# Pooled attention and a token/channel mixer on one core: the head and all step plans in a new order

## The chip, the cores and the metric

The kernel runs on one core of one Trainium2 chip. A core has five engines that run side by side, each working through its own instructions in program order: TensorE (PE, matmuls), VectorE (DVE), ScalarE (ACT), GpSimd (POOL) and SyncE (SP, which here only issues DMAs). They wait for each other through semaphores. Matmul results go to PSUM (eight banks), everything else lies in SBUF. The metric is the device time of one execution in microseconds (us); the median of three runs stands for a kernel.

## The reference

Attention over keys and values that are averaged over 8 neighbours, then a mixer over the sequence and one over the channels:

```python
# q, k, v: (8, 8, 576, 64) = batch, heads, sequence, head size
k_p = k.reshape(B, H, S // 8, 8, D).mean(axis=3)          # 72 pooled keys
v_p = v.reshape(B, H, S // 8, 8, D).mean(axis=3)
attn = softmax(q @ k_p.T / sqrt(D))                       # 576 x 72 for each head
x = (attn @ v_p)                                          # to (8, 576, 512): batch, sequence, channels
h = relu(x.T @ w_tok1) @ w_tok2                           # over the sequence: 576 -> 256 -> 576
u = x + h.T
out = u + relu(u @ w_ch1) @ w_ch2                         # over the channels: 512 -> 1536 -> 512
```

## The kernel before

**What is computed where.** A batch is 576 rows of 512 channels: four chunks of 128 rows, and a tail of 64 that two batches share. The last stage, over the channels, is cut into nine *units*: unit n takes the four full chunks of batch n (n = 0 to 7), unit 8 all the tails. A unit (`unit_fast`) is first 12 tiles of u @ w_ch1 (`l1_tile`, 4 matmuls of 128x512 each, then a ReLU on ACT into `GT`), then seven products with w_ch2, 12 matmuls of 128x256 each, in which the 2x2 blocks of the matrix product are combined from fewer products with the help of sums: `=1` to `=4` (`g_sums`, sums of halves of `GT`) and `w0` to `w3` (`weight_sum`, sums of halves of w_ch2, once, in unit 0). The sums are single DVE instructions of 128x1536. Each product is read out of PSUM by DVE (`plus`); an output is stored by SP.

**The steps of a batch.** While unit n runs, the attention and the token mixer of the batches after it are worked in, as small steps (`batch_steps`):

- `lk`, `lv`, `lq`: the loads of K, V and Q, DMAs that POOL issues (two, two and one).
- `K0`, `K1`, `V0`, `V1`: pooling of four heads on POOL, three instructions each; `v1` is the same on DVE; `kpool`, `vpool0`, `vpool1` are the same by matmuls with an identity, read out by DVE.
- `Q0`, `Q1`: transposes of Q on DVE. `kpT`: transposes of the pooled keys on PE, read out by ACT.
- `s0`, `s1`, `s2`: scores (16 matmuls, in two PSUM buffers of the pool `ps_two`), then two exponentials on ACT.
- `av0` to `av4`: weighted values (8 matmuls in one buffer of `ps_two`), then a reciprocal and a product on DVE; `av4` is the tail.
- `at0`, `at1`: first half of the token mixer, 5 matmuls, ReLU on ACT. `u0` to `u4`: second half, 2 matmuls (4 in `u4`), plus x on DVE.
- For batches 0 to 2 `t0` to `t3` turn u over on PE, and ACT reads it out. For batches 3 to 7 this goes through memory instead: `M0`, `M2`, `M4` write pairs of chunks to memory, `M` (four DMAs) and `MT` (two) read them back in another layout, all issued by SP, and `T0` to `T5` finish with a transpose on DVE.

`l1_tile`, `at`, `u`, `kpT`, `t`, the pooling by matmul and the products take their PSUM bank from one list of four (`take`, `give`): a bank goes to whoever is next in program order, and that one waits until the former reader is done.

**What sets the order.** The order of all instructions is written out by hand in two tables. `HEAD` is the list of steps before unit 0: the first loads (`LkA` to `Lc2c`: parts A, B and T of K and V of batch 0, Q, the weights t1, t2, c1 and c2, and batch 1), batch 0's attention by finer steps (`kp`, `kt`, `q`, `o`, `e`, `a`, `m`: pooled keys, their transposes, queries, odd and even scores, weighted values, token mixer), `p0` and `p1` (a permutation of w_tok2 on ACT and on POOL), and `d1` to `d4`, which are one to four spare matmuls of 128x512 whose result nobody reads. `PLAN` has one dictionary for each unit: a unit has 45 slots (24 half tiles of `l1_tile`, 21 thirds of a product), and after slot i the steps listed under i are issued. Position in the table sets the place in the queue of every engine that the step uses; engines don't wait for each other because of it, only for data.

**Gates.** `g` in a plan is a one-element memset on DVE and a one-element copy of it on POOL. So POOL goes no further until DVE has come there; and since the next memset overwrites what the copy reads, DVE at the next gate waits until POOL has done the copy of the gate before.

```python
def gate():
    nc.vector.memset(flag[:, 0:1], 0.0)
    nc.gpsimd.tensor_copy(out=flag[:, 1:2], in_=flag[:, 0:1])

def unit(n, at):
    ...
    for i, _ in enumerate(unit_fast(n, st)):
        for s in at.get(i, "").split():
            ...
```

In the lists after the heading of the change, `2.K1` under 27 in the first dictionary means: step K1 of batch 2, after slot 27 of unit 0.

Of the kernel before, what the change touches and what calls it, by code (L numbers as in the profile page):

```python
# [32 lines left out]


# [745 lines left out]
```

## Time and profile before

| | |
|---|---|
| median of three runs | 271.05 us (268.42 to 271.4) |
| the profiled execution, its own time | 269.83 us |
| its span, first to last instruction | 268.0 us |
| mean granted TensorE clock | 0.998 |
| first matmul, last product's start | 1.19 us, 263.06 us |
| unit 0's first l1 matmul | 27.18 us |
| DMA traffic of the core | 34.29 MB, 128 GB/s on average, some 200 GB/s until 59 us |

The profile is of one execution. A row of the timeline has the start, the length, the engine, the line of the kernel, the operation, what is written from what, the shape and the count; in brackets stand the idle time of the engine just before and what ended it. Names of tiles leave out buffer numbers: `p1a` to `p1d` are the four banks of the list, `p` a buffer of `ps_two`, `area` the `GT` sums, `flag` the gate, `mem` the memory that batches 3 to 7 go through and `v` what is read back from it. The lines: L514 is an l1 matmul and L518 its ReLU, L580 a product and L623 its readout, L542 and L554 the sums, L297 scores and L306 their exponentials, L376 an `av` with L380 and L381 on DVE, L390 an `at`, L407 and L412 `u` with L413 on DVE, L421 a `t`, L222 `kpT`, L174 to L180 pooling, L118 and L128 loads, L431 spills, L443 the reads back and L455 the DVE transposes, L676 a spare matmul, L709 and L710 the gate.

### The profile page before, as it was taken

What the parts mean: (1) busy time and instruction counts of PE and PEld (TensorE: products, weight loads), DVE (VectorE), ACT (ScalarE), POOL (GpSimd) and SP (SyncE); (2) the same over time, 40 slices, a digit from 0 to 9 for tenths busy, and PEclk for the clock granted to TensorE, in tenths of its full rate; (3) what the DMA queues carried; (4) which work ended last, traced back from release to release, by engine and by line L of the source; (5) the groups of instructions that cost most, each with busy time, mean ns of one, the idle gap of its engine ahead of it and who ended that gap; (6) DMA issues with size and microseconds to landing.
All of it is one profiled execution on the core that took longest, in us unless ns stands there. A gap on an engine that the chain in (4) does not pass through costs nothing. (4 is left out here: it accounts for less than half of the span.)

```text
span 268.0 us, 5292 instructions
## 1 busy us (share of the span) xinstructions
PE 254.6 (95%) x2091; PEld 159.1 (59%) x2113; DVE 177.7 (66%) x368; ACT 119.4 (45%) x196; POOL 148.3 (55%) x175
## 2 busy tenths in 40 slices
PE   7788999989989999999998999999999999999994
PEld 3674366754647645674486347754774486486483
DVE  5476359986699654994879836952796577175183
ACT  2454674039545556415740474265525412612700
POOL 8585324899997999899935892598400001000000
PEclk9999999999999999999999999999999999999999
DMA  7999999992099817699539721370326052603204
GB/s 153 189 206 201 206 206 208 207 201 57 2 150 155 170 36 148 142 217 235 175 85 167 203 81 39 43 205 0 116 45 158 30 163 48 156 0 88 71 0 157
DMA packets 31704, 34.29 MB, mean 128 GB/s; under 512 B 3136, under 2 KB 23744, under 8 KB 31680
## 3 DMA queue, kind: packets, MB, share of 16 engines
q0 software_dynamic: 17632, 17.64, 41.3%
q1 hardware_dynamic: 13632, 15.93, 20.7%
q10 hardware_dynamic: 416, 0.39, 0.4%
q8 instruction: 16, 0.26, 0.4%
q14 instruction: 8, 0.07, 0.1%
HBM read 38.99 MB, written 12.58 MB: 192 GB/s over the span
## 5 line engine op out<-in xcount | busy, mean ns | idle before, releaser
L514 PEld LDWEIGHTS <-w_ch 128*128 128x128 bf16 x432 | 39.3, 98 | 43.9 <-issue 3.2
L710 POOL COPY flag<-flag 1x1 f32<-1x1 f32 x45 | 10.8, 240 | 88.7 <-DVE flag L709 88.5
L580 PEld LDWEIGHTS <-area 128*128 128x128 bf16 x432 | 40.9, 98 | 9.4 <-issue 2.7
L306 ACT ACTIVATE ex<-p 72x768 bf16<-72x768 f32 x42 | 31.6, 806 | 22.5 <-PE p L297 22.5
L580 PEld LDWEIGHTS <-GT 128*128 128x128 bf16 x324 | 30.9, 98 | 7.8 <-issue 1.3
L175 POOL TENSOR_TENSOR t<-t 72x512 f32<-72x512 f32 x23 | 31.3, 1359 | 1.8
L514 PE MATMUL p1a<-uT,w_ch 128*128 128x512 bf16 x104 | 28.5, 379 | 0.3 <-issue 0.2
L518 ACT ACTIVATE GT<-p1a 128x512 bf16<-128x512 f32 x30 | 18.0, 599 | 19.4 <-PE p1a L514 19.3
L514 PE MATMUL p1d<-uT,w_ch 128*128 128x512 bf16 x95 | 25.8, 379 | 0.3
L174 POOL TENSOR_TENSOR t<-kr 72x1024 f32<-72x1024 bf16 x12 | 25.5, 2123 | 0.4
L518 ACT ACTIVATE GT<-p1d 128x512 bf16<-128x512 f32 x28 | 16.8, 599 | 17.7 <-PE p1d L514 11.7
L514 PE MATMUL p1c<-uT,w_ch 128*128 128x512 bf16 x87 | 24.2, 379 | 0.4 <-issue 0.2
L174 POOL TENSOR_TENSOR t<-vr 72x1024 f32<-72x1024 bf16 x11 | 23.3, 2118 | 0.5 <-DMA vr<-in_v_dram 0.3
L518 ACT ACTIVATE GT<-p1b 128x512 bf16<-128x512 f32 x24 | 14.4, 599 | 18.9 <-PE p1b L514 17.7
L514 PE MATMUL p1b<-uT,w_ch 128*128 128x512 bf16 x83 | 22.3, 379 | 0.1
L518 ACT ACTIVATE GT<-p1c 128x512 bf16<-128x512 f32 x26 | 15.6, 600 | 13.8 <-PE p1c L514 12.8
L381 DVE TENSOR_TENSOR x<-p,den 128x512 bf16<-128x512 f32 x28 | 19.4, 692 | 1.0
L376 PEld LDWEIGHTS <-ex 72*128 72x128 bf16 x280 | 13.3, 98 | 7.5 <-DVE x L381 2.1
L376 PE MATMUL p<-vp,ex 72*128 72x65 bf16 x280 | 14.9, 194 | 1.1 <-DVE x L381 0.8
L554 DVE TENSOR_TENSOR area<-GT 128x1536 bf16<-128x1536 bf16 x9 | 8.7, 963 | 9.4 <-ACT GT L518 9.3
L118 POOL DMA_DIRECT2D kr<-in_k_dram x17 | 11.0, 650 | 5.0 <-DMA w_ch<-in_moe_w_ch_dram 1.7
L455 DVE STREAM_TRANSPOSE uT<-v 128x256 uint32<-128x256 uint32 x20 | 8.2, 429 | 7.2 <-DMA v<-mem 7.2
(173 smaller groups left out, 464.2 us busy)
## 6 DMA issues: line engine op xcount, KB each, us to landing
out_dram<-o SPq DMA_DIRECT2D x32, 256.0 KB, 3.6
qb<-in_q_dram POOLq DMA_DIRECT2D x7, 576.0 KB, 8.9
kr<-in_k_dram POOLq DMA_DIRECT2D x7, 512.0 KB, 7.5
vr<-in_v_dram POOLq DMA_DIRECT2D x7, 512.0 KB, 12.3
w_ch<-in_moe_w_ch_dram POOLq DMA_DIRECT2D x5, 512.0 KB, 14.9
mem<-u SPq DMA_DIRECT2D x10, 256.0 KB, 2.2
v<-mem SPq DMA_DIRECT2D x20, 128.0 KB, 2.9
area<-in_q_dram SPq DMA_DIRECT2D x2, 288.0 KB, 3.1
```

Source lines behind the costliest of these rows:

```text
L118: nc.gpsimd.dma_start(out=t[j0:j1, h0:h1].rearrange("j h i d -> j h (i d)"), in_=src[b, h0:h1].rearrange("h (j i) d -> j h (i d)", i=POOL) ...
L174: eng.tensor_tensor(out=t4[:, 0:n], in0=t[:, hs, 0:4], in1=t[:, hs, 4:8], op=ALU.add)
L175: eng.tensor_tensor(out=t4[:, 0:n, 0:2], in0=t4[:, 0:n, 0:2], in1=t4[:, 0:n, 2:4], op=ALU.add)
L306: nc.scalar.activation(out=dst, in_=src, func=AF.Exp, scale=scale)
L376: nc.tensor.matmul(out=ps[:, h // 4, (h % 4) * (D + 1):(h % 4 + 1) * (D + 1)], lhsT=st["ex"][:, h * S + n0:h * S + n0 + P], rhs=st["vp"][: ...
L381: nc.vector.tensor_tensor(out=dst.rearrange("p (a h d) -> p a h d", a=2, d=D), in0=view[:, :, :, 0:D], in1=den[rows, :, :, None].broadcast ...
L455: nc.vector.transpose(out=dst.rearrange("f k n -> f (k n)").bitcast(U32).rearrange("f (k o a t) -> f o a k t", k=4, o=4, a=2)[:, o], in_=s ...
L514: nc.tensor.matmul(out=ps, lhsT=w_ch1[:, kk, m * P:(m + 1) * P], rhs=uT[kk], start=(kk == 0), stop=(kk == 3))
L518: nc.scalar.activation(out=GT[:, m, :], in_=ps, func=AF.Relu)
L554: nc.vector.tensor_tensor(out=S4[:, 0], in0=GT[:, f, hi], in1=GT[:, sec, hi], op=ALU.add)
L580: nc.tensor.matmul(out=ps[i] if split else ps[:, i], lhsT=chunk(u, i, a(m)), rhs=w(m), start=start and m == 0 and (i == 0 or split), stop= ...
L710: nc.gpsimd.tensor_copy(out=flag[:, 1:2], in_=flag[:, 0:1])
```

## The change

Both tables get new contents; no other line differs. `HEAD` has the same steps in another order, with 17 instead of 19 spare matmuls (12 instead of 14 of them ahead of the first step that needs K, `kp1`): LvT goes ahead of LkB, Lt2 ahead of LvB and Lt1, Lc1a and Lc1b ahead of Lk1 and Lq1, Lc2a ahead of Lc1d; kp0 and kp2 go ahead of their former neighbours kt1 and o1, o2 and p0 change places with others, and the `m`, `u` and `t` steps have a new order. `PLAN` has the same steps of each batch and the same sums in each unit, at other slots; 3.lk goes to the very start of unit 0, and the number of gates of units 1 to 8 goes from 4, 5, 6, 4, 5, 7, 6, 2 to 5, 6, 4, 4, 9, 11, 2, 1 (unit 0 has 6 in both).

```diff
--- before.py
+++ after.py
@@ -18,17 +18,17 @@
 SYNC = mybir.EngineType.SP
 
 
-HEAD = """LkA LkT LkB Lq LvA LvT LvB Lt1 Lt2 Lk1 Lq1 Lc1a Lc1b Lc1c p1 Lv1 Lc1d Lc2a Lc2b Lc2c d2 d3 c1 prep c0 d1 d2 d4 q1 d2 q0 kp1 kt1 kp0 o1 kp2 e1 kt0 kt2 o0 q3 e0 q2 d1 e3 o2 vpool0 e2 a02 a00 vpool1 o3 a04 a10 m03 m01 p0 m04 a12 m02 m10 m11 a14 m00 d1 m13 m12 m14 u1 u3 d2 u2 t1 u0 d1 t3 t2 t0 1.kpool"""
+HEAD = """LkA LkT LvT LkB Lq LvA Lt2 LvB Lt1 Lc1a Lc1b Lk1 Lq1 p1 Lc1c Lv1 Lc2a Lc1d Lc2b Lc2c c1 d3 d2 d2 prep d4 q1 c0 d1 q0 kp1 kp0 kt1 kp2 o1 kt0 e1 kt2 q3 o0 e0 q2 e3 vpool0 o3 e2 d2 a02 p0 a00 vpool1 o2 a04 d1 a10 m03 m04 a12 m01 d1 m02 m11 a14 m00 m10 m13 m12 m14 u3 u0 u1 d1 u2 t3 t0 t1 t2 1.kpool"""
 PLAN = [
-    {0: "2.lk 2.lv", 1: "1.kpT", 2: "1.Q1", 5: "1.Q0", 6: "1.s0", 10: "1.s1", 11: "g 1.vpool0", 12: "2.lq =3", 13: "3.lq 1.s2", 14: "1.vpool1", 15: "1.av1", 16: "1.av0 g", 17: "1.av2", 19: "1.av3", 20: "1.av4 w0", 22: "g", 23: "=1", 24: "1.at1 3.lk w1", 25: "=2", 26: "3.lv =4 1.at0 g w3", 27: "2.K1", 30: "2.K0", 31: "1.u0", 33: "g 1.u2", 34: "1.u1", 35: "w2", 37: "1.t0", 39: "1.u3", 41: "2.Q0", 42: "1.t3 2.V0", 43: "1.t1 1.t2", 44: "1.u4 g 2.kpT 2.Q1"},
-    {1: "3.Q0", 2: "2.s0", 3: "3.Q1", 6: "2.s2", 8: "3.K0", 11: "2.s1", 14: "3.K1", 15: "2.v1", 17: "2.av3", 18: "2.av0", 19: "2.av4", 21: "g 4.lq 2.av1", 22: "2.av2", 24: "5.lk g", 25: "3.V1 =1 =2 2.at0", 26: "3.kpT", 27: "2.at1", 29: "3.s0 2.u3 4.lk 2.u1", 30: "2.u2 4.Q0", 31: "3.s2", 32: "4.lv", 33: "2.t3", 34: "=4 g =3", 35: "2.u0", 36: "3.s1", 39: "2.t2", 40: "3.V0", 42: "2.t1 2.t0", 43: "g", 44: "3.av4"},
-    {1: "4.K0", 2: "g", 3: "3.av0 4.Q1 g", 4: "4.K1", 5: "3.av3", 9: "6.lk", 10: "3.av1", 11: "3.av2 g", 13: "4.V0 =3 3.at0", 14: "4.V1", 15: "3.at1", 16: "4.kpT 3.u0", 17: "3.u2 4.s2", 19: "3.u3", 21: "3.u1", 22: "3.M2", 23: "6.lq", 24: "3.M0 =1 5.lq", 25: "5.lv", 26: "3.M =2", 27: "g", 30: "4.s1", 31: "3.u4", 32: "4.s0 =4", 34: "3.T1", 35: "g", 36: "3.T0", 38: "6.lv", 39: "3.T3 4.av4 3.T2", 40: "4.av1", 41: "3.M4", 42: "4.av0", 44: "3.MT 5.Q0"},
-    {0: "4.av2", 4: "5.K1", 5: "5.K0", 6: "4.av3", 7: "g", 9: "5.Q1 4.at1", 10: "4.at0 5.kpT", 12: "4.u0 4.u2", 13: "6.Q0 5.s0", 14: "5.V0 4.u3", 16: "5.V1 4.M2", 17: "4.u1", 18: "=3", 19: "3.T5", 20: "3.T4", 21: "4.M0", 23: "=1 5.s1", 24: "g", 25: "=2 4.M", 27: "5.av1 g", 29: "7.lk", 30: "4.T1", 31: "4.T2 g", 32: "5.s2", 33: "=4", 34: "5.av0", 36: "7.lq", 37: "g 5.av3 g", 38: "5.av2", 40: "4.T3 5.av4", 43: "4.T0", 44: "5.at0 5.at1"},
-    {1: "6.Q1 5.u0 6.K0", 2: "6.K1", 3: "5.u1", 5: "5.u2 g 5.u4", 8: "g", 10: "5.u3", 13: "6.V1 5.M0", 14: "6.kpT 7.Q0", 15: "g", 17: "6.s0", 19: "5.M2 5.M", 20: "7.Q1", 23: "5.T3", 25: "=1 =2", 28: "6.s2", 29: "=4 5.T1 5.T2 6.V0", 32: "=3 5.T0", 33: "g", 36: "6.s1", 39: "7.lv", 43: "6.av4", 44: "6.av2"},
-    {2: "6.av0", 7: "7.K0", 11: "7.K1 g 6.av3", 13: "6.av1", 14: "g 7.V0", 15: "6.at1 6.at0", 18: "6.u0 6.u1", 19: "7.kpT", 20: "g", 22: "6.u3 7.V1 6.u2 7.s0", 25: "6.M2 6.M0", 26: "=1", 28: "=2 7.s1", 29: "=4", 30: "g", 32: "7.av1", 34: "g 6.M", 35: "6.T2", 36: "=3 6.T0", 37: "7.s2", 38: "6.T1", 39: "6.T3", 42: "7.av4", 44: "7.av3"},
-    {1: "g", 2: "g 7.av0", 7: "7.av2", 10: "7.at1", 12: "7.at0", 14: "7.u1", 15: "7.u3 =3 7.u0", 16: "g", 17: "7.u2", 19: "g", 20: "7.u4", 22: "7.M0", 23: "g =1", 24: "=2", 28: "7.M4 7.M2", 29: "=4", 34: "7.M", 37: "7.T3 g", 38: "g 7.T0", 39: "7.T1", 40: "7.T2", 43: "7.MT"},
-    {0: "g", 6: "g", 10: "g g", 12: "7.T5", 17: "g", 21: "g", 22: "7.T4", 23: "=1", 26: "=2", 32: "=4", 37: "=3"},
-    {2: "g", 20: "=3", 23: "=1", 25: "=2", 26: "g", 29: "=4"},
+    {0: "1.Q0 g 2.lk 1.Q1 3.lk", 1: "2.lv", 2: "1.kpT", 3: "g", 4: "1.s0", 6: "2.lq", 8: "1.s1", 9: "1.vpool1", 10: "1.vpool0", 11: "=3 1.s2", 14: "1.av1", 15: "1.av0", 17: "1.av2 w0", 19: "g 1.av3", 20: "1.av4 g", 23: "3.lq", 24: "=1 1.at0 =2", 25: "=4", 27: "w1 3.lv", 28: "g w3 1.at1", 31: "1.u1", 32: "2.K1", 33: "1.u2 1.u0", 34: "w2", 36: "2.K0", 37: "1.t0", 38: "2.V0", 39: "1.u3", 40: "1.t2", 41: "1.t3", 42: "g 1.t1", 43: "2.Q0", 44: "2.Q1 1.u4"},
+    {0: "2.kpT", 1: "3.Q1", 2: "2.s0", 3: "3.Q0", 6: "2.s2", 7: "g", 8: "2.v1", 10: "4.lq 3.K0 g", 12: "2.s1", 13: "3.K1", 18: "2.av3", 19: "4.lk 2.av0", 21: "2.av1", 22: "5.lk 2.av2", 23: "2.av4", 24: "=1 =2", 25: "2.at0 2.at1", 26: "3.kpT g =4", 27: "3.V1", 28: "2.u1", 29: "3.s0 2.u2", 30: "2.u3", 31: "4.lv 2.u0 4.Q0 3.s2", 33: "2.t2", 34: "g", 35: "=3", 37: "2.t3 3.s1", 41: "3.V0", 42: "2.t1 2.t0", 43: "g", 44: "3.av0 4.Q1 3.av1"},
+    {0: "4.K0", 1: "6.lq", 5: "3.av4", 7: "g", 8: "3.av3", 10: "3.av2 4.V1 4.K1", 12: "3.at0 3.at1", 14: "3.u0", 17: "3.u3", 18: "3.u2", 19: "3.M2 4.V0 g 5.lv", 20: "3.u1", 21: "=3", 22: "4.kpT", 23: "=1 5.lq", 24: "4.s1", 26: "3.M0 3.u4", 27: "4.s0 g", 28: "3.M 3.M4 =2", 29: "6.lv =4 3.T0", 30: "g", 32: "4.s2", 35: "3.T2 3.T3 3.MT", 36: "3.T1", 37: "6.lk", 38: "g", 39: "g", 40: "4.av4", 41: "4.av2", 43: "4.av1"},
+    {0: "5.K0", 1: "6.Q0 5.K1", 4: "5.V0 5.Q1", 5: "4.av0", 7: "4.av3", 10: "4.at0", 13: "5.V1 5.kpT 4.at1 =3", 14: "g", 15: "4.u3 5.Q0", 16: "4.u2", 21: "3.T4 5.s0 7.lk 4.u1", 23: "3.T5 4.u0 =1", 24: "g 4.M0 5.s1", 25: "=2", 27: "g", 28: "5.av1", 29: "=4", 31: "5.s2", 33: "g", 34: "5.av0", 35: "5.av3", 36: "4.M2", 37: "4.M", 38: "4.T3 5.av2", 40: "5.av4", 41: "4.T0 4.T2", 42: "7.lq", 43: "4.T1 5.at0", 44: "5.at1 7.Q0"},
+    {3: "5.u1", 6: "6.K1", 7: "6.K0", 8: "5.u3", 9: "6.kpT", 11: "5.u2", 14: "5.u0 6.V0 g", 15: "5.M2", 16: "=3", 18: "6.s0", 19: "5.M0", 20: "6.V1", 21: "6.Q1 5.M", 23: "=1", 25: "=2", 26: "6.s2 g", 27: "5.T1", 28: "5.T0 =4", 34: "6.s1", 35: "g", 36: "g", 37: "7.Q1", 38: "5.T3", 39: "5.T2", 40: "6.av4", 44: "6.av1 5.u4 6.av2"},
+    {1: "7.lv", 4: "7.K1", 7: "7.K0 g", 8: "6.av0", 10: "6.av3", 13: "=3 g", 14: "g", 15: "7.V0 6.at1", 17: "g 6.at0", 19: "6.u2", 20: "6.u3 7.kpT", 21: "6.u0 7.s0", 22: "6.u1", 24: "=1", 25: "=2", 27: "7.s1", 28: "6.M0", 29: "=4", 31: "7.V1", 32: "6.M2", 33: "7.s2", 36: "g", 37: "g 6.M", 38: "g 6.T0 6.T2", 39: "6.T3 6.T1", 41: "g", 43: "7.av3", 44: "g"},
+    {2: "7.av1", 3: "g", 4: "7.av0", 5: "7.av4", 7: "7.av2", 9: "g", 10: "7.at0 7.at1", 13: "7.u0 7.u1", 14: "g 7.u2", 15: "g", 16: "7.u4", 17: "7.M0 7.u3 g", 19: "=3", 22: "g", 23: "g =1", 25: "=2", 28: "7.M2", 30: "=4 7.M", 31: "7.T3 g", 33: "7.M4 7.T2", 35: "7.T0", 37: "g", 40: "g 7.T1", 44: "g 7.MT"},
+    {3: "7.T5", 16: "=3", 19: "g", 23: "7.T4", 24: "=1", 28: "=2", 30: "=4", 44: "g"},
+    {8: "g", 12: "=3", 24: "=1", 28: "=2", 30: "=4"},
 ]
 
 
```

## The prediction

> **What bounds the kernel now.** I read the page's engine line first, then the busy time by stage, then TensorE's timeline for its gaps, and last, at each gap, the timeline of the engine that it names.
>
> ```profile
> span 268.0 us, 5292 instructions
> PE 254.6 (95%) x2091; PEld 159.1 (59%) x2113; DVE 177.7 (66%) x368; ACT 119.4 (45%) x196; POOL 148.3 (55%) x175
> ```
>
> TensorE (PE) is busy for 95%: the order around it can only win back its gaps. By stage (the columns are the length, then each engine's busy time, clock, DMA share and GB/s):
>
> ```profile
> 0.00:27.20 27.20, 22.61 (x203) 14.99 (x205) 15.40 (x41) 11.04 (x17) 18.71 (x32) 1.00 1.14 188
> 58.70:89.80 31.10, 29.58 (x281) 17.97 (x286) 23.90 (x38) 19.28 (x32) 28.83 (x29) 1.00 0.58 101
> 117.70:148.40 30.70, 29.50 (x251) 17.79 (x252) 24.01 (x53) 13.33 (x22) 22.63 (x23) 1.00 0.80 166
> 200.00:224.80 24.80, 24.69 (x177) 15.24 (x176) 17.39 (x41) 8.15 (x14) 1.23 (x7) 1.00 0.34 96
> ```
>
> The head (to 27.2) lacks 4.6 us, units 1 and 3 lack 1.5 and 1.2, units 6 and 7 (from 200) almost nothing. The gaps, in TensorE's timeline (start, length, then in brackets the idle time and who ended it):
>
> ```profile
> 58.67 0.30 PE L222 MATMUL p1c<-ident,kp 72*128 72x72 bf16 x4 [1.27 <-POOL kp L178]
> ...
> 79.93 0.60 PE L580 MATMUL p1b<-area,area 128*128 128x256 bf16 x4 [1.16 <-DVE o L623]
> ...
> 142.73 0.43 PE L376 MATMUL p<-vp,ex 72*128 72x65 bf16 x8 [0.83 <-DVE x L381]
> ...
> 144.25 0.43 PE L376 MATMUL p<-vp,ex 72*128 72x65 bf16 x8 [0.21 <-DVE flag L709]
> ...
> 260.41 1.47 PE L580 MATMUL p1c<-w_ch,area 128*128 128x256 bf16 x12 [0.34 <-DVE s L623]
> ```
>
> From start to start each is some 0.17 longer than its bracket, since a 512-column matmul is shown with 0.38 but the next starts after 0.216. So outside the head about 5 us can be won, in four places. Two of them lead to VectorE (DVE):
>
> ```profile
> 74.49 4.00 DVE L542 TENSOR_TENSOR area<-area,GT 128x1536 bf16<-128x1536 bf16 x1
> ...
> 139.51 0.77 DVE L455 STREAM_TRANSPOSE uT<-v 128x256 uint32<-128x256 uint32 x2 [1.37 <-DMA v<-mem]
> ```
>
> ```profile
> 74.16 1.27 POOL L118 DMA_DIRECT2D kr<-in_k_dram  x2
> 75.42 0.17 POOL L710 COPY flag<-flag 1x1 f32<-1x1 f32 x1
> 75.56 2.11 POOL L174 TENSOR_TENSOR t<-vr 72x1024 f32<-72x1024 bf16 x1
> 77.75 1.86 POOL L175 TENSOR_TENSOR t<-t 72x512 f32<-72x512 f32 x1
> ```
>
> The sum `=2` of unit 1 took 4.00 where its like take 0.95, ending only when pooling step 3.V1 passed from its first to its second operation; all evictions behind it were late, and TensorE waited at 79.93 for a bank. In unit 3 a transpose stood at the head of DVE's queue 1.37 before its data had come back from memory, and the evictions behind it cost the waits at 142.73 and 144.25.
>
> **The change, part by part.** The plans hold the same steps before and after: only order and gates differ. A position below is a plain sum of TensorE's steps in program order: half an l1 tile 0.432, a third of a product 0.436, scores 0.56, an `av` 0.26, an `at` 1.08, a `u` 0.43, a `t` 0.22, `kpT` 0.13 (start-to-start in the timeline).
>
> *A. Head, -0.3 (bounds -1.0 and +1.2).* Two spare matmuls fewer, 2 x 0.216 = 0.43, all ahead of the first K data (landed 7.50, used at 7.64): the wait there grows from 1.33 to about 1.76, nothing is won. LvT now goes ahead of LkB, and the identity (two POOL rows, 0.24 and 0.29) too, so LkB is issued at about 3.8, not 2.62, and lands between 9.1 (the small load's 0.28 added to 8.77) and 9.9 (issue plus the 6.15 that it took). kp2 has moved ahead of o1 and meets this load: TensorE is there at 8.8 and waits 0.3 to 1.1. Against it, kp0 fills the wait for kt1's input (0.38 at 8.63 before). ScalarE's chain of eight exponentials (0.59 to 0.70 each) and p0 (1.24) starts 0.5 to 0.9 later but without its gaps; I follow it to a10 at about 17.55 instead of 17.8 and to kpool at about 25.15 instead of 25.45. The other loads: c1a and c1b pass ahead of k1 and q1 (k1 lands near 23.3 instead of 20.65, q1 25.6 instead of 22.93), enough for kpool at 25 and for 1.Q0; c1d trades places with c2a (36.5 for 33.9), and tile 8 of unit 0 wants it near 37.8; t1 and t2 trade places and stay ahead of use. 3.lk goes ahead of 2.lv and 2.lq, each then lands 2.7 later, still before K1, V0 and Q0 of batch 2.
>
> *B. Wait for 2.kpT, -0.7 (bounds -1.5 and 0).* K1 and K0 of batch 2 are a chain of 9.6 from the gate's copy (48.12) to 58.6. kpT moves one slot on (0.43), and w0, formerly queued between the last `av` and `=1`, now stands where DVE has room, which lets the gate come 0.3 earlier. The rest of the wait stays.
>
> *C. Unit 1, -1.4 (bounds -1.5 and 0).* The gate that let 3.V1 start ahead of `=1 =2` is now behind them (slot 26), ahead of `=4`, and V1 at 27. `=2` then meets at most the two issues of 4.lk and 5.lk. If K1's pooling runs late into `=1`, that costs DVE up to 2.1 once, of which some 2 us of slack before product 3 take most. Is it the pooling or the DMA issue that held `=2`? In unit 0 `w1` and `=2` (44.62, 45.49) ran 0.95 beside the same kind of issues, so I take the pooling. The Trainium skill (SBUF — State Buffer, "Who interferes with whom") says that a DVE instruction with two SBUF inputs contends with a GpSimd instruction that reads SBUF, and that the one that issues first has the port to its end. The trace agrees at 131.42 (1.90 for 0.95, started inside a pooling row) and disagrees at 74.49, started 1.07 before the pooling; by the rule `=2` had some other cause to wait, C would be nought and the whole sum -1.8.
>
> *D. Unit 3, -1.3 (bounds -1.4 and 0).* From the end of a batch's last `u` to its first transpose T there were, before, 7.33, 6.46, 6.31, 7.04, 9.25 us (batches 3 to 7), and DVE waited 0, 1.37, 5.10, 0.52, 0.23; only batch 4's and a bit of batch 6's wait reached TensorE, the others stood where nothing was queued. After: 5.71, 8.44, 6.75, 8.09, 6.08. Batch 4's gets longer by 2 and its two gates among the `av`s go.
>
> *E. Units 5 and 8, -0.3 (bounds -0.5 and 0).* Batch 6's 7.04 becomes 8.09 (0.26 lost near 198); in unit 8 DVE runs without a break from 255.56 to 260.36, and one gate (about 0.1) leaves it.
>
> *F. New waits, +0.8 (bounds 0 and 3.6).* Batch 3's T0 stands right behind M. Its data need, after u1's end, 0.8 for the eviction, some 2.1 for the spill and 4.4 for four reads (108.14 to 112.5): 7.3, and DVE, which has `=2`, an eviction and `=4` ahead of T0, reaches it at about 7.4. The loads 5.lv and 5.lq start just then; each 1 us later delays the evictions behind by as much, with 2.5 to spare before product 6 reads its bank. If the data are 6 later, that is 3.6. V0 of batch 3 ends only 0.85 before av0 wants it, K1 of batch 4 (now behind V1) 1.6 before kpT. 7.Q0 is queued on DVE about 7 us after 7.lq can be issued; qb loads took 8.1 there: DVE waits 1, in a stretch where only u1 stands behind it and banks are free: nothing.
>
> Gates that DVE has to wait for (a gate needs POOL's copy of the one before) cost 0.9 in all before; the new ones in units 5 and 6 stand where POOL has little left: nothing, 0.3 each if POOL were late.
>
> Sum: -0.3 - 0.7 - 1.4 - 1.3 - 0.3 + 0.8 = -3.2 us. The profiled execution took 269.83 (268.0 span and 1.83 around it): 266.6. It lies 1.2 under the median of the runs, 271.05; on that, 267.8.
>
> **The rivals.** *R1, given back:* what held `=2` stays, or the next late thing (a K chain, the LkB load, a collision of a sum with pooling in another unit) takes its place. For it: of 40 sums four were stretched, by 3.05, 0.32, 0.47 and 0.95, and every new order draws anew. Against it: the new gates mostly stand behind the sums. -1.8 to 0; about 270.
>
> *R2, slower:* the transposes. Batches 3, 5 and 7 have distances of 5.71, 6.75 and 6.08, all under the 7.33 that was the shortest with no wait. If reads come back as the pair at 119.46 did (9.9 instead of 4.4), DVE stands as long as the 5.10 seen at 163.0 in each; less the 2.8 that fit before the next bank is needed, 3 x 2.3 = 6.9 lands on TensorE: 267.8 + 6.9 = 274.7. It decides once reads take more than about 7. Against it: 5.10 cost nothing before, and units 4 and 6 have no `av` near.
>
> *R3, more:* the head takes its good bound, F is empty: -0.3 becomes -1.0 and +0.8 becomes 0, -4.7; about 266 and below.
>
> **How the numbers follow.** Forecast 0.52, R1 0.26, R2 0.17, R3 0.05. The runs of before spread over 3 us, so about 1% is what a measurement tells from no change: faster means under 268.3, slower over 273.8. The forecast's own range is 265.5 to 269.5, some 0.40 of it faster and 0.12 within 1%; R3 is faster; R1 is within 1% but for 0.02. Faster 0.45, same 0.36, slower 0.19. The range goes from 264.5 (all gains at their bounds, -5.9, give 265.2, and the runs' spread) to 273, leaving out most of R2.
>
> **What would show it.** A: kp2 starts at 9.2 to 10, kpool near 25. B: kpT of batch 2 still waits for POOL, 0.4 to 0.9. C: `=1 =2` of unit 1 at 0.95 each, no gap at unit 1's products. D: no DMA wait of a T in unit 3 with an `av` gap behind. F: DVE's wait at T0 in unit 2 under 2 us. I am wrong if a sum is stretched by 3 us again, or if a gap over 1 us stands in units 2 to 6 where there was none.

## The result and the profile after

The changed kernel took 284.36 us (median of 4 runs, 281.62 to 287.29) against 270.16 for the kernel before on the same chip: ratio 1.0496, 95% interval 1.0385 to 1.0608. It is 5% slower, where 267.8 was forecast. Ratios, here and below, are of the executions within 1.5% of the fastest of their kernel, which leaves out the 287.29. The profiled execution took 281.62, the shortest of the four. The page's engine line and its row of clocks:

```profile
span 279.8 us, 5310 instructions
...
PE 259.9 (93%) x2111; PEld 161.2 (58%) x2111; DVE 180.7 (65%) x371; ACT 119.4 (43%) x196; POOL 151.0 (54%) x178
...
PEclk9999999999999999869999599999999999999999
```

The clock row shows two dips that the page of before does not have. Unit starts (first l1 matmul of each in TensorE's timeline) say where the 11.8 us of longer span lie:

| | head | unit 0 | 1 | 2 | 3 | 4 | 5 | 6 | 7 | 8 to the end |
|---|---|---|---|---|---|---|---|---|---|---|
| before | 27.18 | 31.63 | 31.03 | 27.87 | 30.71 | 24.57 | 27.10 | 24.69 | 19.53 | 23.71 |
| after | 26.91 | 30.26 | 31.61 | 35.49 | 36.60 | 24.72 | 26.05 | 25.12 | 19.53 | 23.51 |

At the start of unit 2 the changed kernel is 1.06 ahead; units 2 and 3 lose 7.62 and 5.89. (A difference of a few tenths in one unit can be a step that moved to its neighbour: an `av` is 0.26.) The busy time by stage, cut at these starts (length, then PE, PEld, DVE, ACT and POOL busy, clock, DMA share, GB/s):

```profile
57.20:88.80 31.60, 30.54 (x297) 18.28 (x296) 27.21 (x40) 19.17 (x32) 30.55 (x30) 1.00 0.63 111
88.80:124.30 35.50, 30.14 (x244) 18.16 (x241) 21.83 (x44) 13.07 (x21) 27.24 (x28) 0.90 0.76 151
124.30:160.90 36.60, 31.60 (x255) 18.49 (x253) 24.01 (x51) 13.43 (x22) 30.13 (x27) 0.91 0.52 104
```

In each of the two units TensorE lacks 5 us, and its clock averages 0.90 and 0.91. Unit 1 is there for comparison, at full clock. TensorE's timeline has the wait for 2.kpT shrunk, a new small one at 68.76, and one long gap in each of the two units:

```profile
58.09 0.30 PE L222 MATMUL p1a<-ident,kp 72*128 72x72 bf16 x4 [0.31 <-POOL kp L178]
...
68.76 0.29 PE L376 MATMUL p<-vp,ex 72*128 72x65 bf16 x4 [0.75 <-DVE flag L709]
...
118.39 1.01 PE L580 MATMUL p1d<-w_ch,area 128*128 128x256 bf16 x4 [5.37 <-DVE s L623]
...
156.53 1.01 PE L390 MATMUL p1d<-x,w_tok 128*128 128x512 bf16 x2 [5.00 <-DVE x L381]
```

Both long gaps lead to DVE, which stood at a transpose (T) of data read back from memory, with the readout that TensorE needs queued behind it. (The row at 74.40 is the sum `=2` of unit 1, for part C below.)

```profile
74.40 1.48 DVE L542 TENSOR_TENSOR area<-area,GT 128x1536 bf16<-128x1536 bf16 x1
...
117.28 0.45 DVE L455 STREAM_TRANSPOSE uT<-v 128x256 uint32<-128x256 uint32 x1 [6.51 <-DMA v<-mem]
117.65 0.69 DVE L623 TENSOR_TENSOR s<-p1d,u 128x512 f32<-128x512 f32 x1
...
155.22 0.45 DVE L455 STREAM_TRANSPOSE uT<-v 128x256 uint32<-128x256 uint32 x1 [5.70 <-DMA v<-mem]
...
155.79 0.69 DVE L381 TENSOR_TENSOR x<-p,den 128x512 bf16<-128x512 f32 x1
```

Why were the data late? SP's issues of unit 2, and POOL's beside them (the last row is from unit 3):

```profile
107.45 1.80 SPq L443 DMA_DIRECT2D v<-mem  x4
```

```profile
107.85 1.29 POOL L118 DMA_DIRECT2D vr<-in_v_dram  x2
109.14 0.75 POOL L128 DMA_DIRECT2D qb<-in_q_dram  x1
...
110.74 1.27 POOL L118 DMA_DIRECT2D vr<-in_v_dram  x2
...
139.83 1.29 POOL L118 DMA_DIRECT2D kr<-in_k_dram  x2 [0.47 <-issue]
```

The loads 5.lv (107.85) and 5.lq (109.14) were issued among the four reads. The DMA view gives the time from issue to landing, first for these reads (L443, tile `v`), then for the spills of batch 4 in unit 3 (L431, tile `mem`), which were issued right behind 7.lk (the row at 139.83):

```profile
DMA to landing us min/median/max: 2.5/4.7/8.3
```

```profile
L431 SPq DMA_DIRECT2D mem<-u x2: 343/387/431, 140.7 to 141.1; - x2
...
DMA to landing us min/median/max: 6.5/6.7/6.8
```

The reads of batch 4 behind these spills were issued at 147.96 to 149.56, and with the load 7.lq issued 1.5 ahead of them (146.47) they landed after 5.3 to 5.7.

In the trace of before, the reads of unit 2 (issued from 108.14 to 109.50) and the spills of unit 3 (at 129.83 and 131.55) landed after

```profile
DMA to landing us min/median/max: 2.5/2.9/3.0
```

```profile
DMA to landing us min/median/max: 2.0/2.0/2.0
```

and POOL's loads came behind them:

```profile
109.09 1.33 POOL L180 TENSOR_TENSOR vp<-t 72x256 bf16<-72x256 f32 x1
110.37 1.47 POOL L128 DMA_DIRECT2D qb<-in_q_dram  x2
...
138.95 1.29 POOL L118 DMA_DIRECT2D kr<-in_k_dram  x2 [1.16 <-issue]
```

POOL was still pooling until 110.37, when the last read was already issued, and 7.lk was issued five microseconds after the spills had landed. In these rows the difference is whether a spill or read is issued ahead of POOL's loads or behind them; e2 and e3 test that.

Around each gap the clock was halved, from 116.84 to 123.67 and from 154.39 to 161.22 (6.83 us each). Unit 2's lengthening of 7.62 less its gap of 5.37 leaves about 2 us for that, and nowhere else in it does TensorE wait. The other three executions ran at a mean clock of 0.964 to 0.970 against 0.976 in the profile. For the two at 0.964 the difference is, by estimate, one more stretch of 6.8 us at half the clock (0.012 of 282 us is half of that); where it lay no trace shows.

### The profile page after: what moved, and what is told of

The parts are those of the page before. It is cut to its first block, busy times and chain, and to the rows that moved or that the text cites. A ratio compares the mean times of both kernels' runs of the same rounds, so it can differ in the third digit from the quotient of the medians.

```text
span 279.8 us, 5310 instructions
## 1 busy us (share of the span) xinstructions
PE 259.9 (93%) x2111; PEld 161.2 (58%) x2111; DVE 180.7 (65%) x371; ACT 119.4 (43%) x196; POOL 151.0 (54%) x178
## 4 chain that ended last, share of the span: by engine, by line
PE 74%; DMA 11%; DVE 10%; issue 2%; SPq 1%; ACT 1%; POOL 0%; DVEq 0%; POOLq 0%
PE p1a L514 8%; PE p1d L514 7%; PE p1c L514 7%; PE p1b L514 7%; PE p1c L580 6%; PE p1a L580 6%; PE p1b L580 5%; PE p1d L580 5%; DMA v<-mem 5%; DMA mem<-u 4%; PE p L376 3%; DMA kr<-in_k_dram 2%; PE p L297 2%; PE p1d L390 2%; DVE area L542 2%
## 5 line engine op out<-in xcount | busy, mean ns | idle before, releaser
L710 POOL COPY flag<-flag 1x1 f32<-1x1 f32 x48 | 13.8, 287 | 89.7 <-DVE flag L709 89.7
L580 PEld LDWEIGHTS <-area 128*128 128x128 bf16 x432 | 42.0, 100 | 14.1 <-issue 6.9
L514 PE MATMUL p1a<-uT,w_ch 128*128 128x512 bf16 x108 | 29.4, 381 | 0.0
L518 ACT ACTIVATE GT<-p1d 128x512 bf16<-128x512 f32 x27 | 16.1, 598 | 20.5 <-PE p1d L514 20.4
L514 PE MATMUL p1b<-uT,w_ch 128*128 128x512 bf16 x92 | 24.7, 379 | 0.0
L518 ACT ACTIVATE GT<-p1b 128x512 bf16<-128x512 f32 x26 | 15.6, 598 | 17.3 <-issue 9.9
L518 ACT ACTIVATE GT<-p1c 128x512 bf16<-128x512 f32 x25 | 14.9, 598 | 17.0 <-PE p1c L514 17.0
L554 DVE TENSOR_TENSOR area<-GT 128x1536 bf16<-128x1536 bf16 x9 | 10.4, 1157 | 12.3 <-ACT GT L518 12.3
L376 PEld LDWEIGHTS <-ex 72*128 72x128 bf16 x280 | 14.1, 101 | 7.2 <-issue 1.0
L542 DVE TENSOR_TENSOR area<-GT 128x1536 bf16<-128x1536 bf16 x9 | 11.3, 1255 | 7.6 <-ACT GT L518 7.6
```

Source lines behind the costliest of these rows:

```text
L376: nc.tensor.matmul(out=ps[:, h // 4, (h % 4) * (D + 1):(h % 4 + 1) * (D + 1)], lhsT=st["ex"][:, h * S + n0:h * S + n0 + P], rhs=st["vp"][: ...
L514: nc.tensor.matmul(out=ps, lhsT=w_ch1[:, kk, m * P:(m + 1) * P], rhs=uT[kk], start=(kk == 0), stop=(kk == 3))
L518: nc.scalar.activation(out=GT[:, m, :], in_=ps, func=AF.Relu)
L542: nc.vector.tensor_tensor(out=out, in0=a, in1=b, op=ALU.subtract)
L554: nc.vector.tensor_tensor(out=S4[:, 0], in0=GT[:, f, hi], in1=GT[:, sec, hi], op=ALU.add)
L580: nc.tensor.matmul(out=ps[i] if split else ps[:, i], lhsT=chunk(u, i, a(m)), rhs=w(m), start=start and m == 0 and (i == 0 or split), stop= ...
```

## The experiments

Each takes the changed kernel as its base unless the text says so, and was compared with the kernel before on the same chip (medians of before: 269.29 for e1 to e4, 269.06 for e5 to e8, 269.38 for e9 to e11, 268.97 for e12). The two theories at the start: *the loads* (POOL's loads, issued ahead of or among SP's small transfers, delay these) and *the head* (the new order of the first loads costs the time later on).

**e1: the new head alone, with the old plans**

```diff
-HEAD = """LkA LkT LkB Lq LvA LvT LvB Lt1 Lt2 Lk1 Lq1 Lc1a
...
+HEAD = """LkA LkT LvT LkB Lq LvA Lt2 LvB Lt1 Lc1a Lc1b Lk1
...
```

> The new HEAD with the old PLAN. Theory L (the loss comes from loads that POOL issues just ahead of the spills and reads back of batches 3 and 4, so that the DVE transposes wait): nothing of that is in the head; unit 0 starts 0.3 earlier (27.18 to 26.9) and the time is that of before within 1 us, ratio 0.995 to 1.003. Rival H (the new order of the first loads is part of the loss): at least 3 us slower than before, ratio 1.01 or more.

Measured: 270.31 (268.28 to 271.89, 10 runs), ratio 1.0033 (1.0001 to 1.0066), units 2 and 3 27.86 and 30.55 as before. The head is not where the 5% come from. Unit 0 started at 27.37 in this profile, not 0.3 earlier than before. And six of its ten executions ran at a mean clock of 0.985 to 0.994 and took 270.25 to 271.89; the others, at 0.999 and 1.0, took 268.28 to 269.63. Of the 19 runs of before beside them, two were under 0.995.

**e2: the three loads of unit 2 behind the reads**

```diff
-19: "3.M2 4.V0 g 5.lv", 20: "3.u1", 21: "=3", 22: "4.kpT", 23: "=1 5.lq"
+19: "3.M2 4.V0 g", 20: "3.u1", 21: "=3", 22: "4.kpT", 23: "=1"
...
-29: "6.lv =4 3.T0", 30: "g"
+29: "=4 3.T0", 30: "g 5.lq 5.lv 6.lv"
```

> The changed kernel, with the three loads of unit 2 (5.lq, 5.lv, 6.lv) put behind the gate of slot 30, which stands behind T0 on DVE; all else as changed. Theory L: the reads back of batch 3 come back within 3 us each, T0 waits under 1 us, the gap of 5.5 us in unit 2 and the half clock behind it are gone, about 7.5 us less than the changed kernel: 274 on the profile of 281.6, ratio to before 1.02; unit 3 keeps its gap. Rival Q (the transposes stand too early on DVE, the data would be late anyhow): a gap of 3 us or more stays in unit 2, over 278.

Measured: 279.84 (4 runs), ratio 1.039 (1.0353 to 1.0426). The four reads in the DMA view:

```profile
DMA to landing us min/median/max: 2.4/2.8/2.9
```

2.9 at most instead of 8.3, DVE's wait at T0 0.65 instead of 6.51, the gap of 5.37 gone: same program otherwise, so the loads are the cause in unit 2. Unit 3 kept its gap. The time fell by less than expected (279.84, not 274), and the profile shows two reasons: TensorE now waits 2.11 at 120.87, the gate that e4 explains below, with 3.41 us of half clock behind it, so that unit 2 still takes 30.47; and the head ran at half clock for 6.83 us, so that unit 0 started at 29.99.

**e3: the load of unit 3 ahead of the spills**

```diff
-4: "5.V0 5.Q1"
+4: "7.lk 5.V0 5.Q1"
...
-21: "3.T4 5.s0 7.lk 4.u1"
+21: "3.T4 5.s0 4.u1"
```

> The changed kernel, with 7.lk put from slot 21 of unit 3 to slot 4, ahead of 5.V0 on POOL; all else as changed. Theory L: the two spills of batch 4 land in 2 to 3 us instead of 6.5 and 6.8, the gap of 5.2 us in unit 3 and the half clock behind it are gone, about 7 us less than the changed kernel: 274.5, ratio 1.02; unit 2 keeps its gap. Rival Q: a gap of 3 us or more stays in unit 3. Rival S (the spills are late because of the stores or of what unit 2's delay has pushed into them, not because of 7.lk): they still take over 5 us.

Measured: 275.03 (4 runs), ratio 1.023 (1.0171 to 1.029). The two spills landed after 3.6 and 3.9, and with them early the reads were issued (144.12 to 145.47) ahead of 7.lq (146.29) and landed after 2.6 to 3.0. Unit 3 took 29.67 instead of 36.60, a full microsecond less than before the change. That is what part D of the prediction had promised, without the load in the way. Unit 2's gap stayed (a wait of 3.60, with 3.41 us of half clock).

**e4: e2 and e3 together**

> Both moves of loads together. Theory L: both gaps and both stretches of half clock gone; what is left of the change is the head's 0.3, unit 0's 1.4 and unit 5's 1.0 to the good and unit 1's 0.6 to the bad: 266 to 268 on the profile, ratio to before 0.985 to 0.995, faster than both kernels. Rival Q: over 275.

Measured: 270.98 (269.79 to 274.18, 10 runs), ratio 1.0078 (1.0039 to 1.0117). Both gaps and both dips are gone in the profile (268.1 us of span at clock 0.999): against the kernel before on its own chip, a loss of 14.2 us (284.36 less 270.16) is down to 1.7 (270.98 less 269.29) by moving four loads. Theory L's 0.985 to 0.995 it missed. Part of what is left is read from TensorE, DVE and POOL at 117:

```profile
118.09 0.43 PE L376 MATMUL p<-vp,ex 72*128 72x65 bf16 x8 [2.05 <-DVE xt L381]
```

```profile
117.12 0.20 DVE L380 RECIPROCAL den<-p 64x8 f32<-64x8 f32 x1 [2.21 <-issue]
117.13 0.06 DVE L709 MEMSET flag<- 1x1 f32 x1
```

```profile
112.44 0.74 POOL L128 DMA_DIRECT2D qb<-in_q_dram  x1
113.18 2.53 POOL L118 DMA_DIRECT2D vr<-in_v_dram  x4
115.67 1.28 POOL L118 DMA_DIRECT2D kr<-in_k_dram  x2
116.91 0.17 POOL L710 COPY flag<-flag 1x1 f32<-1x1 f32 x1
```

The bracket on DVE names no releaser, but the times do: DVE starts again when POOL's copy of the gate (116.91) ends, and that copy stood behind seven DMA issues of 4.5 us together. Issuing is work for POOL, and a gate makes DVE wait for it.

**e5: the transposes of batch 3 at the end of unit 2, the loads where the change put them**

```diff
-29: "6.lv =4 3.T0"
+29: "6.lv =4"
...
-35: "3.T2 3.T3 3.MT", 36: "3.T1"
+35: "3.MT"
...
-43: "4.av1"
+43: "4.av1 3.T0 3.T2 3.T3 3.T1"
```

> The changed kernel with its loads as changed, but T0, T2, T3 and T1 of batch 3 all put to slot 43 of unit 2, behind the last av. Theory L (late data, and DVE's queue makes them a wait for everybody): the reads land as late as in the changed kernel, near 117, but evictions and avs of unit 2 go on; what stays is a wait of 1.5 to 2.5 us at the start of unit 3, too short for the half clock, so about 5 us less than the changed kernel, 276 to 278. Rival Q (the place on DVE is all there is to it): no wait over 1 us left, 274 or less. Rival N (the data are needed at once, the place does not matter): a wait of 5 us stands at the start of unit 3, 281 or more.

Measured: 274.53 (4 runs), ratio 1.0164 (1.0109 to 1.0218). The third and fourth read still took 7.6 and 9.7 (landed 119.03 and 121.58), and TensorE now waited 3.92 for the first l1 matmul of unit 3 with the clock halved behind it. In unit 2 moving the reader of late data made the gap shorter and put it elsewhere; it is cured at the transfer. The total came out lower than expected, though the wait was longer. The larger part of the saving lies in unit 3, which took 31.95 instead of 36.60, with no gap in it: here POOL came to 7.lk 6.2 us ahead of the spills (136.09 and 142.30), and these landed after 3.6 and 3.8. So this too went by where the load stood.

**e6: 6.lv and 6.lk behind the last gate of unit 2 (on e4)**

```diff
-30: "g 5.lq 5.lv 6.lv"
+30: "g 5.lq 5.lv"
...
-37: "6.lk", 38: "g", 39: "g"
+38: "g", 39: "g 6.lv 6.lk"
```

> Both loads moved as in e4, and in unit 2 6.lv and 6.lk put behind the gate of slot 39 instead of between the gates of slots 30 and 39. Theory G (in e4 DVE stood 2.2 us at the gate of slot 39, because POOL had four load issues of 3.8 us between its copies of two gates): the gap of 2.05 us at 118 is gone, span 266 on an undisturbed clock, 2 us less than e4. Rival: the gap is the av's data, and stays.

Measured: 273.63 (4 runs), ratio 1.0173 (1.0133 to 1.0214). The gap at the gate is gone and unit 2 takes 27.49, but another has come at the start of unit 3:

```profile
126.92 0.24 PE L222 MATMUL p1a<-ident,kp 72*128 72x72 bf16 x2 [2.55 <-POOL kp L178]
```

```profile
114.93 1.24 POOL L118 DMA_DIRECT2D vr<-in_v_dram  x2
116.16 1.25 POOL L118 DMA_DIRECT2D kr<-in_k_dram  x2
117.41 2.15 POOL L174 TENSOR_TENSOR t<-kr 72x1024 f32<-72x1024 bf16 x1
```

The 2.5 us of issues now stand ahead of the pooling of 5.K0 and 5.K1, and TensorE waits for their result as long. The clock was halved from 128.16 to 131.58. So the gate was the cause of e4's gap, but the forecast of 2 us less than e4 failed.

**e7: e6 without the gate at step 7 of unit 1; e8: e7 with the old head**

```diff
-6: "2.s2", 7: "g", 8: "2.v1"
+6: "2.s2", 8: "2.v1"
```

> As e6, and the gate of slot 7 of unit 1, ahead of 2.v1, left out. Theory G: DVE no longer stands 1.9 us at that gate until POOL has pooled 2.V0, v1 runs from 61 instead of 63 beside V0, and the av wait of 0.9 us in unit 1 goes: span 265, 0.9 less than e6. Rival P (v1 is slow because it is made beside POOL's pooling, gate or not): V0 and v1 stretch each other, K0 and K1 of batch 3 come later, nothing is gained.

> The plans of e7 with the HEAD of before. Theory C (the new head leaves TensorE idle for 2.3 to 2.7 us ahead of kp1, and in some runs the clock is halved behind that, +2 to +3.5 us): the runs lie close together, within 2 us, clock 0.995 or more in nearly all, median 267, ratio to before 0.99: faster than both kernels. Rival: the spread of e1 and e4 is not the head's, runs with a clock of 0.98 to 0.99 stay at a third or more.

Measured: e7 272.4 (4 runs), 1.0111 (1.008 to 1.0143); e8 271.28 (11 runs), 1.008 (1.0053 to 1.0107). Without that gate DVE begins 2.v1 3.4 us into unit 1 instead of 5.5 and is through at 9.8 instead of 11.5; unit 1 takes 30.66 instead of 31.57. So the 0.75 at 68.76 is the gate's doing. That v1 is stretched beside POOL's pooling is not: it takes 6.4 us in e7, 6.1 in the changed kernel and 3.7 before. In e8 unit 0 starts earliest of all (26.54), but under the old order of loads the V of batch 1 comes too late for the plan's earlier `vpool1` (TensorE waits 1.15 for it). Both keep the gap at 5.kpT (2.84 and 2.55) with 3.41 us of half clock behind it. Theory C of e8 failed: its median is not 267 but 271.28, and seven of its eleven executions had a clock of 0.991 to 0.994. As the half clock in its profile lies at that gap, this says nothing of the head.

**e9: 6.lv and 6.lk behind 5.K1 (on e7); e10: the same with 9 spare matmuls behind `q0`; e11: the old plans with the new head and these 9**

```diff
-39: "g 6.lv 6.lk",
+39: "g",
...
-{0: "5.K0", 1: "6.Q0 5.K1",
+{0: "5.K0", 1: "6.Q0 5.K1 6.lv 6.lk",
...
-d1 q0 kp1
+d1 q0 d9 kp1
```

> The new head and plans, with 5.lq and 5.lv behind the gate at step 30 of unit 2, 7.lk at step 4 of unit 3, the gate at step 7 of unit 1 left out, and 6.lv and 6.lk moved once more: from the gate at step 39 of unit 2 to step 1 of unit 3, behind 5.K0 and 5.K1, which POOL then pools first. Theory G (POOL's loads delay whatever POOL does next, and that is all they do here): 2.kpT's 2.5 us wait of unit 3's start goes, units 2 and 3 take 27.5 and under 30.5 us, the half clock at 128 goes with the gap; with the head at full clock the run is 267 to 268.5 us, with a half clock in the head 270 to 271.5. Rival B (two loads of 6 at once are too late or collide with the spills of batch 4): spills mem<-u of batch 4 take over 4 us and T3 waits, or 6.K waits for its load in unit 4; 271 or more also with the head at full clock.

> The kernel of e9 with 9 spare matmuls more behind q0, where TensorE waits for kp1 in the head. Theory I (the new head lets TensorE idle from its last spare matmul to the transpose of kp1; whether the clock is halved behind that is a matter of the run, and costs 2 to 3 us when it is): with the idle stretch filled no execution shows a half clock in the head, unit 0 starts at 26.9 to 27.6 in the profile, the lowest run clock is 0.995 or more, and the runs spread by under 1.5 us; median 267 to 268.5, ratio 0.992 to 1.000. Rival J (the half clock there has nothing to do with that stretch): clocks of 0.98 to 0.995 stay among the runs and the spread stays 2 to 4 us; median 269 to 271.

> The plans of before with the new head, as e1, and 9 spare matmuls more behind q0. e1 had run clocks of 0.985 to 1.0 with times of 268.3 to 271.9 and a ratio of 1.0033. Theory I: clocks of 0.995 or more in all runs, spread under 1.5 us, ratio 0.996 to 1.000 (unit 0 starts 0.3 earlier than before). Rival J: clocks down to 0.985 again, ratio 1.002 to 1.005.

Measured: e9 272.4 (4 runs), 1.0103 (1.006 to 1.0146); e10 269.32 (12 runs), 1.0005 (0.9977 to 1.0033); e11 270.89 (12 runs), 1.0058 (1.0024 to 1.0092). The wait at 5.kpT is gone, but six DMAs in a row (6.lv, 6.lk and 7.lk) now delay POOL's next work, the pooling of 5.V0 and 5.V1, and the spills behind them. TensorE's timeline and the DMA view of the spills, both of e10:

```profile
137.59 0.31 PE L376 MATMUL p<-vp,ex 72*128 72x65 bf16 x4 [1.91 <-POOL vp L180]
```

```profile
DMA to landing us min/median/max: 2.4/5.5/5.7
```

The two spills landed 5.5 and 5.7 after issue (the 2.4 is a read). So e9's rival had the time and the slow spills right, but what TensorE waited for was POOL, not the spills: DVE asked for the reads behind them late enough.

On the clock in the head the three say less than hoped. With the stretch filled, three of e10's 12 executions and four of e11's were under 0.995, against six of e1's ten; but five of the 23 runs of before were too, and a mean clock does not say where the half clock was: in e10's profile (0.991) it was in unit 3 and at the end. Nor was e11 faster than e1: its profile has a wait of 1.73 in unit 3 (0.83 before) with 3.41 us of half clock behind it, and one of 0.73 in unit 5. The traces alone tell of the head: of nine with the new head as it is, four have a half clock in it (e2, e3, e5, e7), of three with it filled one (e12), of two with the old head none. That an idle TensorE ahead of `kp1` causes the half clock stays likely and unshown.

**e12: e10 with the loads spread, and `vpool` two steps later**

```diff
-1: "6.Q0 5.K1 6.lv 6.lk", 4: "7.lk 5.V0 5.Q1"
+1: "6.Q0 5.K1 6.lk", 4: "5.V0 5.Q1"
...
-33: "g", 34: "5.av0"
+33: "g 6.lv", 34: "5.av0"
...
-26: "6.s2 g", 27: "5.T1"
+26: "6.s2 g 7.lk", 27: "5.T1"
...
-9: "1.vpool1", 10: "1.vpool0", 11: "=3 1.s2"
+11: "=3 1.vpool1 1.s2", 12: "1.vpool0"
```

> The kernel of e10 with the three loads that stood together behind 5.K1 in unit 3 spread by POOL's free time: 6.lk stays behind 5.K1 (step 1 of unit 3), 6.lv goes behind the gate at step 33 of unit 3, 7.lk behind the gate at step 26 of unit 4; and 1.vpool1 and 1.vpool0 go from steps 9 and 10 of unit 0 to 11 and 12. In e10 the 3.78 us in which POOL issued six DMAs (124.52 to 128.30) stood ahead of the pooling of 5.V0 and 5.V1, whose end at 137.53 ended a TensorE wait of 1.91 us, and the spills of batch 4 behind them took 5.5 and 5.7 us. Theory G (a load costs POOL its issue and the DMAs behind it their turn, and what decides is only what stands next on POOL and on SP): with two DMAs instead of six there, 5.V1 is pooled at about 135, before TensorE asks for it at 135.5, the wait of 1.91 is gone or under 0.5, unit 3 takes 30.0 to 31.0 us instead of 32.92, the spills take 1.7 to 3.5 us; unit 4 stays at 24.5 to 25.0. With unit 0 at 30.3 to 31.0, span 265.3 to 267, time 267 to 268.7, ratio to before 0.992 to 0.998. Rival K (the new plans leave POOL or the DMAs no room for these loads wherever they stand): the wait comes back elsewhere, 6.V0 or 7.K waits for its load in unit 4 or 5, or the reads of batch 4 take over 4 us; ratio 1.000 or more.

Measured: 268.37 (12 runs), ratio 0.9967 (0.9948 to 0.9985): faster than the kernel before by a third of a per cent, which the interval just tells from nothing, and 5% faster than the changed kernel by the two ratios (0.9967/1.0496 = 0.950). Theory G's ranges for the time, the ratio, unit 3 and the spills all held. (The later `vpool` steps answer a wait of 1.11 that e10's profile has for the V of batch 1, as e8's has.) Its profiled execution is one with the head at half clock (unit 0 starts at 30.91), so it is read from unit 0's start on: 238.3 us to the end, against 240.8 before and 252.9 after the change. Unit 3 takes 30.35; its only wait over half a microsecond is

```profile
140.56 0.53 PE L297 MATMUL p<-qD,kD 32*72 32x192 bf16 x14 [0.84 <-DVE x L381]
```

and the spills and reads around it landed after 2.6 to 3.3.

## Why the prediction was wrong, point by point

*A, head:* right in its number, -0.3 forecast, -0.27 measured (unit 0 at 26.91), but by luck. kp2 started at 9.55 and kpool at 25.18, as said; the wait ahead of the first K matmul was 2.39, not 1.76; and the five profiles with the new head at full clock have unit 0 at 26.76 to 27.37, the two with the old one at 27.18 and 26.54, so that 0.27 is within their scatter. Left out was the clock: e1 has the new head at +0.3%, not -0.1%, most likely because more of its executions run a few microseconds at half clock.

*B, 2.kpT:* better than forecast. Of the wait of 1.27 there remains 0.31, so 0.96 is won instead of 0.7. (Unit 0's 1.37 is more because the step and what is left of its wait now stand in unit 1.)

*C, unit 1:* the cause was right, the gain was given back. `=1` took 0.94 and `=2` 1.48 (0.95 was forecast), and TensorE has no gap at the products. That the pooling held `=2`, and not the issues, fits what came next: `=2` began while POOL was still in the last operation of K1 (73.02 to 75.06), and `=4`, at 76.45, took 0.95 within the issues of 4.lk and 5.lk (75.01 to 77.57). By the rule of the Trainium skill (SBUF — State Buffer, "Who interferes with whom") that the prediction quotes, the 4.00 would have stayed. One reading was off: before, `=2` did not end as 3.V1 passed to its second operation (77.75) but 0.7 later, at 78.49, and that operation took 1.86 where its like take 1.26. What gave the gain back is the new gate ahead of 2.v1, which held DVE for 1.9 where the prediction priced only those of units 5 and 6; v1 then ran stretched beside POOL's pooling (its second operation 3.41, before 1.65), and TensorE waited 0.75. e7 shows this wait to be the gate's. Net, unit 1 lost 0.58 where 1.4 was to be won, some of it for steps that moved in (2.kpT and one `av` more). This is R1's mechanism.

*D, unit 3:* wrong. Batch 4's distance of 8.44 from `u` to T was taken as enough, because 6.46 had cost only 1.37. The step moved 7.lk ahead of the spills of batch 4, and the prediction, which followed the loads of units 0 and 2, did not follow this one on POOL's queue. With 6.5 to 6.8 for the spills and 5.3 to 5.7 for the reads even 8.44 fell 5.70 short. The reads came behind 7.lq because the spills were late. With 7.lk out of the way (e3) D's gain is there.

*E:* unit 5 got 1.05 shorter, but three `av`s left it for units 4 and 6; the three units together gained 0.47, against 0.26 forecast. Unit 8's gap went from 0.34 to 0.16.

*F, new waits:* this is the step that failed. It saw the place ("The loads 5.lv and 5.lq start just then") and the consequence, but priced the reads at the 4.4 that they took before, for +0.8. That price belonged to an order in which POOL's first load was issued at 110.37, after the last read; here it was issued 0.40 after the first. The top end of F, 6 us of delay for 3.6, came near in the delay (6.51 of wait on DVE) but took 2.5 as spare; TensorE's gap was 5.37, so only 1.1 was. And it had no term for the clock, another 2 us behind each long gap. Unit 2's term was +7.6 and unit 3's +5.9, where F and D together had -0.5. The trace of before had the price for reads behind loads: those of MT (four in the trace, not two, at 119.46 to 121.89, each of 64 KB), issued while POOL's loads of 110.37 to 114.76 were still landing, took 7.4 to 8.5. The prediction used them for R2 alone.

*Rivals:* R2 named the mechanism and the point from which it decides ("once reads take more than about 7"; from first issue to last landing they took 9.7 at batch 3 and 7.1 at batch 4), but got the batches wrong: it put the stalls at 3, 5 and 7 by the distances alone, and they came at 3 and 4, by where POOL's loads stood. At batches 5 to 7 DVE waited for no read of M; its one wait there, 4.51 at 242.77 for the tails' read (MT), was 4.97 before and cost TensorE nothing in either. Its evidence against ("5.10 cost nothing before") was true of a wait with nothing queued behind it. A chance of 0.17 at a price of 6.9 was too little on both counts, and the loss of 14 lies outside every case. The last sentence of the text, a gap over 1 us in units 2 to 6, was the sign that came.

## What to carry to other kernels

When an order written by hand moves a load, follow that load on its issuing queue past every small transfer of another queue that something waits for: a duration from the old trace holds only for the old neighbours on the DMAs. Put large loads behind the short round trips through memory, and where the issuing engine has nothing urgent next, since the issues cost it time as well (0.6 to 0.75 us each here). And price a TensorE gap by more than its length, because the clock may halve around it: here that came with waits from 1.73 to 5.37 us.

## What the runs showed of the hardware that was not expected

- Small transfers that SP issues behind or among POOL's loads are slowed by a multiple: 128 KB reads from 2.5 to 3.0 up to 8.3 us (9.7 in e5), 256 KB spills from 2.0 to 6.5 and 6.8. The Trainium skill (DMA: Bandwidth & Descriptors, "Queues, rings and completion order") says that a DMA engine takes turns between its queue rows, a packet at a time. The DMA view agrees for the reads of unit 2: from 110.5 to 117.2 POOL's queue moved 808 packets and SP's 611, but 0.96 MB against 0.39, so that SP's transfers got under a third of the bytes. For the spills of unit 3 it shows something else: from 140.7 to 145.0 POOL's queue moved 0.43 MB and SP's none at all, and from 145.0 to 148.0 SP's moved 0.52 MB. What held the spills is not known.
- The clock was halved for 3.41 or 6.83 us, and not only at long gaps: in e6 behind a wait of 2.55, in e10 behind one of 1.91 (from 137.72 on), in e11 behind one of 1.73, while 2.05 in e4's profile brought none. The Trainium skill (TensorE: Matmul & The Clock Gate, "What's actually happening") gives a window of 3.4 us that runs freely, with the clock halved after an idle one. The lengths of 3.41 and 6.83, one window and two, agree with it; the waits of 1.73, 1.91 and 2.55, each shorter than a window, do not.
- The ten executions of e1 spread over 3.6 us and those of e4 over 4.4, on one chip, and most of it goes with the mean clock (0.98 to 1.0). Whether a short idle stretch halves the clock seems to be a matter of the execution: at the same gate, e2's profile has a wait of 2.11 and a half clock behind it, e4's a wait of 2.05 and none. The kernel before spreads less (2.0 us over the 19 executions beside e1 and e4).
